# Five numbers and one condition in the virtual clock of a fused S4D and MLP-mixer kernel

## The chip, the cores and the metric

The kernel runs on one core of a Trainium2 chip. That core has a matrix engine (TensorE, called PE in the profile), a vector engine (VectorE, DVE), a scalar engine (ScalarE, ACT), GpSimd (POOL) and a queue engine (SyncE, SP), each with its own instruction stream; they meet at semaphores only. DMAs are issued from SP, ACT and POOL. The metric is the device time of one execution in microseconds, as the median of several runs.

## The reference

```python
xn = _layernorm(x)                              # x: 2048 tokens x 576 channels
s  = irfft(rfft(xn^T) * rfft(K))^T + xn * D_skip   # K: S4D kernel, 576 channels, 128 states, 2048 long
h  = gelu_tanh(_layernorm(xn) @ w1 + b1)        # 576 -> 4608
g  = silu(h @ w2 + b2)                          # 4608 -> 576
return x + s * g
```

Everything is fp32, and the channel convolution is as long as the sequence.

## The kernel before, in words

There are two bodies of work. The MLP ("mlp") is cut into 48 slots. The 4608 hidden features form 12 groups of 384, the 2048 tokens form four blocks of 512; the first half of the kernel takes the token blocks 0 and 1 through all 12 groups, the second half the blocks 2 and 3. A slot is one group for one block of 512 tokens. It has 11 positions on PE: three tiles of layer 1 (L619, 14 matmuls of 512 columns each, since every fp32 product is made of three fp32r products of high and low parts), and eight positions of layer 2 (L682; 12, 6, 6, 12, 18 and 18 matmuls of 288 columns in the order of the trace, 72 in all). Behind each layer 1 tile ACT makes Gelu (L655), ACT rounds it to the high part `hh` (L658) and DVE subtracts to get the low part `hl` (L661); layer 2 reads both. Layer 2's sums are added into `acc` by DVE (L692).

The second body is the S4D convolution ("s4d"). 36 steps make the convolution's kernel: tables of sines and magnitudes on ACT and DVE (L917 to L957; the two sines of a step are L934 and L936), then 64 small matmuls on PE ("KG", L996). Six chunks of 96 channels are then convolved by transforms: "X1" (L1108, twice a chunk), "K1" (L1139, twice), "S2" (the second stage, L1167, four times), "INV" (the inverse step, L1210, twice) and "I1" (L1236, once), with ACT and DVE work between them. I1's result goes to DRAM (`s_s`, L1245).

At the end the output x + s*g is made in two ways. For tokens of blocks 0 and 1, `combine_load` (L721 to L723) brings u, s and g back in `row` tiles by three POOL DMAs, `combine` multiplies and adds on DVE (L729, L730), and POOL issues the stores (L733). This is done in two rounds: one for the first 384 channels when four of the six chunks are done, and one for the last 192 channels in three sets (three, three and two blocks of tokens) when the last chunk is done; the sets follow one another in one line of steps. For blocks 2 and 3, `finish` works straight from `acc` in the last two slots: ACT (L765), then DVE (L770 or L772 and L776, then L780), then the store (L782). `row` tiles have four buffers.

The order of all instructions on all engines is made while the program is traced, by the class `Order`, a list scheduler with a virtual clock. Its clock has one time per engine (`t`). Work on PE of the MLP is placed by `unit`; all other work stands in "lines", each a queue of `step`s with an engine, a duration, marks that it needs and perhaps a latest start (`by`). `advance` runs, up to the PE clock, whatever can start earliest. A step of a line may run only if it ends before the next urgent step of its engine has to start (`soon`, from the `by` times of Gelu, `hh`, `hl` and `acc`, which `hidden_by`, `add_by` and `look_ahead` work out from the list `LEN` of the durations of a slot's positions). An urgent step itself (Gelu and what follows it, and the evacuation of a KG that rode with another unit) isn't tested. ACT's functions need tables: Gelu and tanh one, the sines another, exp and sqrt others. `take` adds 1.28 to a step that has to change the table; the test in `advance` adds 1.28 or 2.56 for a step that itself needs a table. A load of a table is an instruction on ACT (ACT_TABLE_LOAD) in the trace. A step with no engine stands for a DMA; its duration is the time after which the next step of its line may start.

The S4D units are put between MLP positions by `pe_turns`, at set places of a slot, when the virtual clock has their inputs ready. Units of X1, K1, S2 and I1 are spread out: `END = 1000.0` is the virtual time at which the last is to be placed, and the number of units left sets the gap between them. A KG whose inputs are ready rides with such a unit (`ride`). Between slots, a "pair" of two half-height matmuls (L602) may take the place of one matmul in each of the first and third tile.

The durations of the planner are constants: X1 (used for X1 and K1), S2, INV, I1 and KG at L1026, L1 (one layer 1 tile, three for each slot) at L1354, and the waits of DMA steps, among them the one of `combine_load` at L1519.

Of the kernel before, what the change touches and what calls it, by code (L numbers as in the profile page):

```python
# [19 lines left out]
NT = 16  # L20
# [19 lines left out]
def dve(n):  # L40
    return 0.075 + 0.00104 * n
# [10 lines left out]
class Order:  # L52
# [85 lines left out]
    def advance(self, horizon):  # L138
        while True:
            best = None  # L140
            soon = dict(self.next)
            for u in self.urgent:
                st = u[1][0]
                k = (max(u[0], self.t[st["eng"]]), 0)
                if u[0] <= horizon and (best is None or k < best[0]):
                    best = (k, u, None)
                for st in u[1]:
                    soon[st["eng"]] = min(soon.get(st["eng"], 1e9), st["by"])
            for x in self.lines:
                if x["steps"] and x["steps"][0]["by"] < 1e9:  # L150
                    st = x["steps"][0]
                    soon[st["eng"]] = min(soon.get(st["eng"], 1e9), max(st["by"], self.t[st["eng"]] + st["dur"]))
            for n, x in enumerate(self.lines):
                h = self.head(x)
                if h is None or h[0]["eng"] == "PE":
                    continue
                st, r = h
                if st["eng"] is None:
                    k = (max(r, 0), 1 + n)
                    if r > horizon:  # L160
                        continue
                else:
                    e = st["eng"]
                    b = max(self.t[e], r)
                    d = st["dur"]
                    if st["tbl"]:
                        d += 1.28 * (1 + (st["tbl"] != self.tbl))
                    if b > horizon or b + d > soon.get(e, 1e9) + st["late"]:
                        continue
                    k = (b, 1 + n)  # L170
                if best is None or k < best[0]:
                    best = (k, None, x)
            if best is None:
                break
            if best[1] is not None:
                self.go(best[1])
            else:
                self.run(best[2])
            self.pin()
# [26 lines left out]
def step(eng, dur, fn, need=(), mark=None, cv=0, at=0.0, late=0.0, tbl=None, by=1e9):  # L206
    return dict(eng=eng, dur=dur, fn=fn, need=tuple(need), mark=mark, cv=cv, at=at, late=late, tbl=tbl, by=by)
# [3 lines left out]
def mixer_kernel(ctx, tc, u, log_a_real, a_imag, c_real, c_imag, log_dt, d_skip, w1, b1, w2, b2,  # L211
# [394 lines left out]
    def layer1(g, tb, i):  # L606
        h, lo, r1, r2 = W[1]
        c = slice(i * P, (i + 1) * P)
        if i < 2 and i not in BEGUN:
            Q1[i] = bank2(mx(i))  # L610
        q = Q1[i % 2][:, i // 2]
        ops = []
        for a, b in ((h, XH), (h, XL), (lo, XH)):
            ops += [(a[:, kb, c], b[:, kb, tb]) for kb in range(KB)]
        ops.append((r1[:, c], XR[:, tb]))
        if i not in BEGUN:
            ops.append((r2[:, c], XR[:, tb]))
        for j, (a, b) in enumerate(ops):
            nc.tensor.matmul(q, a, b, start=j == 0 and i not in BEGUN, stop=j == len(ops) - 1, skip_group_check=True)  # L619
        return hidden(g, tb, i, q)  # L620

    def first_layer1(i):


        h, lo, r1, r2 = W[1]
        if i != 1:
            Q1[i] = bank2("mxb" if i else "mxa")
        q = Q1[2][:, 0] if i == 2 else Q1[0][:, i]
        pairs = [(h, XH, 0), (h, XH, 1), (h, XL, 0), (h, XH, 2), (h, XL, 1), (h, XH, 3), (h, XL, 2), (h, XL, 3)]

        if i != 1:
            for j, (a, b, kb) in enumerate(pairs):
                for k in ((0, 1), (2,))[i // 2]:
                    nc.tensor.matmul(Q1[k // 2 * 2][:, k % 2], a[:, kb, k * P:(k + 1) * P], b[:, kb, 0],
                                     start=j == 0, stop=False)
        c = slice(i * P, (i + 1) * P)
        for kb in range(KB):
            nc.tensor.matmul(q, lo[:, kb, c], XH[:, kb, 0], start=False, stop=False)
        for r in (r1, r2):
            nc.tensor.matmul(q, r[:, c], XR[:, 0], start=False, stop=r is r2)  # L640

        return [hidden(0, 0, k, Q1[k // 2 * 2][:, k % 2]) for k in ((), (0, 1), (2,))[i]]
# [75 lines left out]
    def combine_load(b, n, c0, c1):  # L718
        m = c1 - c0
        r = [sb.tile([P, D], F32, name="row", bufs=NROW)[:, :n * m].rearrange("p (i d) -> p i d", i=n) for _ in range(3)]  # L720
        nc.gpsimd.dma_start(r[0], u_s[:, b:b + n, c0:c1])  # L721
        nc.gpsimd.dma_start(r[1], s_s[:, b:b + n, c0:c1])
        nc.gpsimd.dma_start(r[2], g_s[b:b + n, :, c0:c1].rearrange("i p d -> p i d"))  # L723
        XS[b] = r

    def combine(b, n, c0, c1):

        x, s, g = XS[b]
        nc.vector.tensor_mul(s, s, g)  # L729
        nc.vector.tensor_add(x, x, s)  # L730
        for i in range(n):
            for y, o in enumerate(rows_at(out, b + i, c0, c1)):
                nc.gpsimd.dma_start(o, x[64 * y:64 * y + 64, i])  # L733
# [289 lines left out]
        return behind  # L1023


    X1, S2, INV, I1, KG = 1.5, 1.75, 2.15, 3.05, 1.03  # L1026

    def chunk(c):

# [242 lines left out]
    el, wl2, wl, nl2, pl, pl2, nl, ml, ml2, xl, wx, c3, c2, c1, c4, kl, tl, sl, vl, gl, odl, fl = [od.line() for _ in range(22)]  # L1272
# [78 lines left out]
    od.pin()  # L1351


    L1 = 14 * 0.2315  # L1354
    LEN = [L1] * G + [3 * n * 0.132 + 0.02 for n in (4, 2, 2, 4, 3, 3, 3, 3)]

    T0 = 12.5
# [96 lines left out]
    def wmark(n, which):  # L1454

        per = KB + 1 + G
        a = n * per + (0 if which == 1 else KB + 1)
        return [("w", k) for k in range(a, a + (KB + 1 if which == 1 else G))]
# [23 lines left out]
    for k in range(8):  # L1482
        gl["steps"].append(step("POOL", 0.7, lambda k=k: part.update({k: load_f2(k)}), mark=("f2", k),
                                need=[("f2c", k - 2)] if k > 1 else ["turns"]))
        fl["steps"].append(step(None, 4.5, lambda: None, need=[("f2", k)]))
        for f in range(2):
            fl["steps"].append(step("ACT", act(256), lambda k=k, f=f: part[k](f), mark=("f2c", k) if f else None,
                                    need=[("f2s", k - 1)] if k and k % 2 == 0 else []))
# [26 lines left out]
    def end_line():  # L1515
        for c, c0, c1, sets in ((NCH - 3, 0, CE, [(b, 1) for b in range(8)]), (NCH - 1, CE, D, [(0, 3), (3, 3), (6, 2)])):
            for b, n in sets:
                a = (b, n, c0, c1)
                ml["steps"].append(step(None, 10.0, lambda a=a: combine_load(*a), need=[("st", c), ("u", NT - 1)]))  # L1519
                ml["steps"].append(step("DVE", 2 * dve(n * (c1 - c0)), lambda a=a: combine(*a)))  # L1520
                ml["steps"].append(step(None, 4.0, lambda: None))

# [46 lines left out]
    later(mid - 2, G, lambda: (parts_in(0), turn_in(1)))  # L1569
    later(mid - 1, G, lambda: parts_in(1))  # L1570
    later(NSLOT - 10, 4, end_line)
    later(NSLOT - 2, 0, lambda: wx["steps"].append(step(None, 0.0, load_identity)))
    for k in range(8):
# [40 lines left out]
    for slot in range(NSLOT):  # L1614
# [5 lines left out]
        for pos in range(NPOS):  # L1620
            if pos < G:
                need = wmark(n, 1) + [("x", tb)]
                if pos == 0:
                    od.force(lambda: all(m in od.marks for m in need))

                    if slot in (1, 2 * NG + 1):
                        od.marks["x", tb] -= 2.3
                cell = []
                od.unit(lambda: cell.extend([layer1(g, tb, pos)] if slot else first_layer1(pos)),
                        L1 * (14 - (pos in BEGUN)) / 14 if slot else L1 * (22, 6, 14)[pos] / 14, need)  # L1630
                if pos == 2:
# [16 lines left out]
            else:  # L1648
                j, terms, last, hid = l2_terms(pos - G)
                need = [wmark(n, 2)[i] for i in hid] + [("h", slot, i) for i in hid]  # L1650
# [17 lines left out]
                elif last:  # L1668
                    add = cell[0]
                    chain = [step("DVE", dve(D), lambda: add(0, 2), mark=("acc", slot, j), by=add_by(pos, j))]  # L1670
                    if final:
                        x = el if slot < NSLOT - 1 else od.line()
                        st = finish(b, 0, D, slot == NSLOT - 1, nc.gpsimd if slot == NSLOT - 1 and j > 1 else nc.sync)
# [69 lines left out]
```

## Time and profile before

| what | value |
|---|---|
| median of 3 runs | 1102.57 us (1101.76 to 1102.64) |
| the profiled execution's own time | 1102.84 us |
| its span, first to last instruction | 1101.0 us |
| granted TensorE clock, mean | 0.999 |
| PE busy | 1090.1 us |
| DVE busy | 892.8 us |
| ACT busy | 725.7 us |
| Gelu's table loads (at L655) | 39 |
| table loads at L934 and L936 | 27 and 7 |

A row of the timeline has the start in us, the busy time, engine, line and operation, output and input, the count, and in brackets the idle time before it with what ended it. A row of the waits has the engine and line that waited, what it waited for, the total in us, the number of times and the longest. Matmuls are pipelined: consecutive matmuls of 288 columns start 0.13 us apart, though each is listed with 0.29 us, so a late start is read from the distance of two starts.

### The profile page before, as it was taken

The numbers are of one execution on the slowest core, as the hardware profiler recorded it, in microseconds if no ns is written. First come the engines' busy times: TensorE is split into PE (matmuls) and PEld (weight loads), VectorE is DVE, ScalarE is ACT, GpSimd is POOL, SyncE is SP. The second block draws the span as 40 slices with busy tenths as digits, with TensorE's granted clock in tenths as the row PEclk, the third lists the DMA queues.
The fourth block names the chain that finished last, engine by engine and source line by source line (L and its number), as shares of the span: only waits on it lengthen the run. The fifth ranks groups of instructions, "written<-read, shape, count | busy, mean of one in ns | idle before, by whom it ended". The sixth has DMA issues, their size and how long they took to land.

```text
span 1101.0 us, 27023 instructions
## 1 busy us (share of the span) xinstructions
PE 1090.1 (99%) x11445; PEld 954.5 (87%) x11445; DVE 892.8 (81%) x1298; ACT 725.7 (66%) x1109; POOL 184.1 (17%) x255
## 2 busy tenths in 40 slices
PE   9999999999999999999999999999999999999997
PEld 7989899898888898888888888888888888888897
DVE  7798677979888889889997988988798986666356
ACT  6585699876848685586947669577666766335233
POOL 4566201071110100001100010000100012110320
PEclk9999999999999999999999999999999999999999
DMA  8846755745542333344723334242333425563543
GB/s 227 236 147 152 236 160 193 214 87 150 160 147 75 67 97 95 99 103 128 169 58 90 85 89 100 53 119 64 92 76 91 146 64 163 131 179 100 161 129 87
DMA packets 139649, 138.22 MB, mean 126 GB/s; under 512 B 88952, under 2 KB 105016, under 8 KB 138952
## 3 DMA queue, kind: packets, MB, share of 16 engines
q1 hardware_dynamic: 124664, 85.49, 29.7%
q0 software_dynamic: 14384, 50.27, 14.7%
q8 instruction: 89, 1.46, 0.6%
q10 hardware_dynamic: 480, 0.74, 0.3%
q14 instruction: 32, 0.26, 0.1%
HBM read 102.17 MB, written 36.63 MB: 126 GB/s over the span
## 4 chain that ended last, share of the span: by engine, by line
PE 87%; DVE 4%; ACT 3%; DMA 2%; SPq 2%; issue 1%; POOL 0%; ACTq 0%; DVEq 0%; POOLq 0%
PE mxb L682 19%; PE mxa L682 19%; PE mxb L619 18%; PE mxa L619 18%; PE cv L1167 3%; PE cv L996 3%; PE cv L1210 2%; PE cv L1139 1%; PE cv L1108 1%; PE cv L1236 1%; SPq L810 1%; DMA row<-g_s 1%; DMA w<-in_A_u_dram 1%; SPq L385 1%; ACT h L655 0%
## 5 line engine op out<-in xcount | busy, mean ns | idle before, releaser
L661 DVE TENSOR_TENSOR hl<-h,hh 128x512 fp32r<-128x512 f32 x144 | 98.7, 688 | 104.1 <-ACT hh L658 103.8
L682 PE MATMUL mxa<-w2h,hh 128*128 128x288 f32 x573 | 171.2, 299 | 2.0 <-DVE acc L692 1.0
L682 PE MATMUL mxb<-w2h,hh 128*128 128x288 f32 x576 | 171.3, 297 | 0.0
L682 PE MATMUL mxb<-w2h,hl 128*128 128x288 f32 x576 | 170.6, 296 | 0.6 <-DVE hl L661 0.5
L682 PE MATMUL mxa<-w2h,hl 128*128 128x288 f32 x573 | 169.2, 295 | 0.4 <-DVE hl L661 0.4
L682 PE MATMUL mxb<-w2l,hh 128*128 128x288 f32 x576 | 169.5, 294 | 0.0
L682 PE MATMUL mxa<-w2l,hh 128*128 128x288 f32 x573 | 168.6, 294 | 0.0
L682 PEld LDWEIGHTS mxa<-w2h,hh 128*128 128x128 f32 x573 | 107.6, 188 | 9.8 <-issue 4.2
L655 ACT ACTIVATE h<-mxa,b1t 128x512 f32<-128x512 f32 x73 | 50.1, 687 | 94.8 <-PE mxa L619 93.6
L682 PEld LDWEIGHTS mxb<-w2h,hh 128*128 128x128 f32 x576 | 108.1, 188 | 4.9 <-issue 1.8
L682 PEld LDWEIGHTS mxb<-w2h,hl 128*128 128x128 f32 x576 | 108.1, 188 | 1.6 <-DVE hl L661 1.5
L682 PEld LDWEIGHTS mxb<-w2l,hh 128*128 128x128 f32 x576 | 108.2, 188 | 0.7
L682 PEld LDWEIGHTS mxa<-w2l,hh 128*128 128x128 f32 x573 | 107.6, 188 | 0.6
L682 PEld LDWEIGHTS mxa<-w2h,hl 128*128 128x128 f32 x573 | 107.5, 188 | 0.6 <-DVE hl L661 0.6
L692 DVE TENSOR_TENSOR acc<-mxa,acc 128x576 f32<-128x576 f32 x87 | 65.3, 751 | 36.4 <-PE mxa L682 36.2
L898 POOL DMA_DIRECT2D par<-par_s x36 | 27.5, 765 | 394.6 <-DVE mg L942 317.9
L658 ACT ACTIVATE hh<-h 128x512 fp32r<-128x512 f32 x144 | 90.8, 631 | 3.7
L655 ACT ACTIVATE h<-mxb,b1t 128x512 f32<-128x512 f32 x71 | 48.8, 687 | 65.3 <-PE mxb L619 62.7
L692 DVE TENSOR_TENSOR acc<-mxb,acc 128x576 f32<-128x576 f32 x88 | 66.1, 751 | 19.5 <-PE mxb L682 19.3
L619 PE MATMUL mxa<-XH,w1h 128*128 128x512 f32 x284 | 78.3, 398 | 0.0
L619 PE MATMUL mxb<-XH,w1h 128*128 128x512 f32 x280 | 77.9, 400 | 0.0
L619 PE MATMUL mxa<-XL,w1h 128*128 128x512 f32 x284 | 76.1, 390 | 0.0
(266 smaller groups left out, 2481.5 us busy)
## 6 DMA issues: line engine op xcount, KB each, us to landing
raw<-in_B_w_dram SPq DMA_DIRECT2D x72, 288.0 KB, 3.5
raw<-in_B_w_dram SPq DMA_DIRECT2D x96, 192.0 KB, 3.5
par_s<-A POOLq DMA_DIRECT2D x4, 2160.0 KB, 9.0
par<-par_s POOLq DMA_DIRECT2D x36, 240.0 KB, 3.7
f2t<-f2q SPq DMA_DIRECT2D x24, 256.0 KB, 3.3
g2t<-g2p SPq DMA_DIRECT2D x24, 256.0 KB, 3.8
bias<-XR SPq DMA_DIRECT2D x42, 128.0 KB, 3.5
raw<-in_B_w_dram SPq DMA_DIRECT2D x48, 96.0 KB, 3.6
```

What stands on the lines that cost most here:

```text
L385: queue.dma_start(XT[b], tok(u, b))
L619: nc.tensor.matmul(q, a, b, start=j == 0 and i not in BEGUN, stop=j == len(ops) - 1, skip_group_check=True)
L655: nc.scalar.activation(t, q, AF.Gelu_apprx_tanh, bias=b1t[:, k:k + 1], scale=1.0)
L658: LAST[0] = nc.scalar.activation(hh[:, i], t, AF.Copy)
L661: nc.vector.tensor_sub(hl[:, i], t, hh[:, i].bitcast(F32))
L682: nc.tensor.matmul(q[:, dh, :288], a[:, i, c], b[:, i, d], start=i == 0 and k == 0 and not alone, stop=i == G - 1 and k == 2)
L692: nc.vector.tensor_add(o, q[:, dh:dh + n, :288], b)
L810: nc.sync.dma_start(r[32 * g:32 * g + 32].rearrange("c (b n) -> c b n", n=32), dram(src[k], 32 * g, [[N, 32], [32 * N, D // 32], [1, 32]]))
L898: nc.gpsimd.dma_start(PAR[b].rearrange("p (g i) k -> p g (i k)", g=4), dram(par_s, (b // 3 * 48 + b % 3 * 4) * NPAR, [[D * NPAR, P], [12 * ...
L996: nc.tensor.matmul(q[32 * g:32 * g + 32, i // 2, i % 2 * 64:i % 2 * 64 + 64], U[:, ri, 4 * g + i, :], v[:, ri, 4 * g + i, :], start=ri == ...
L1167: nc.tensor.matmul(Q[i][32 * q:32 * q + 32, f, ri::2], m[r, 4 * i + q, 32 * ri:32 * ri + 32], A2[r, 4 * p + 2 * i + q // 2, :, :, q % 2], ...
L1210: nc.tensor.matmul(QI[q // 2][64 * f:64 * f + 64, q % 2, i], MAT["g2t", p + i // 2][r, i % 2, f, ri], YS[p + i // 2][0][r, i % 2, ri, f], ...
```

## The change

The condition: the test of a step of a line on ACT that itself needs no table counts 1.28 more while the table in the virtual clock isn't Gelu's. The numbers: X1 1.50 to 1.48, S2 1.75 to 1.73, INV 2.15 to 1.98, KG 1.03 to 1.04; a matmul of layer 1 from 0.2315 to 0.2275, thus a tile from 3.241 to 3.185; and the wait behind `combine_load` from 10 to 13.

```diff
@@ -165,6 +165,8 @@
                     d = st["dur"]
                     if st["tbl"]:
                         d += 1.28 * (1 + (st["tbl"] != self.tbl))
+                    elif e == "ACT" and self.tbl != "gelu":
+                        d += 1.28
                     if b > horizon or b + d > soon.get(e, 1e9) + st["late"]:
                         continue
@@ -1023,7 +1025,7 @@
-    X1, S2, INV, I1, KG = 1.5, 1.75, 2.15, 3.05, 1.03
+    X1, S2, INV, I1, KG = 1.48, 1.73, 1.98, 3.05, 1.04
@@ -1351,7 +1353,7 @@
-    L1 = 14 * 0.2315
+    L1 = 14 * 0.2275
     LEN = [L1] * G + [3 * n * 0.132 + 0.02 for n in (4, 2, 2, 4, 3, 3, 3, 3)]
@@ -1516,7 +1518,7 @@
-                ml["steps"].append(step(None, 10.0, lambda a=a: combine_load(*a), need=[("st", c), ("u", NT - 1)]))
+                ml["steps"].append(step(None, 13.0, lambda a=a: combine_load(*a), need=[("st", c), ("u", NT - 1)]))
```

No instruction's shape or operands change; what changes is the order in which the instructions stand on the engines, and what follows from it. The two added lines move the line numbers behind L167 by two; this text keeps the numbers from before.

## The prediction

> **What bounds the kernel now.** First the page: the span and the engines' busy time.
>
> ```profile
> span 1101.0 us, 27023 instructions
> PE 1090.1 (99%) x11445; PEld 954.5 (87%) x11445; DVE 892.8 (81%) x1298; ACT 725.7 (66%) x1109; POOL 184.1 (17%) x255
> ```
>
> PE is busy all but 10.9 us. So the time is PE's own stream of matmuls, plus its late starts, plus a tail after the last matmul. Then the waits of PE:
>
> ```profile
> PE mxa L1298 <- POOL XL L1291: 1.3, 1, 1.3
> PE mxa L682 <- DVE acc L692: 1.0, 1, 1.0
> PE mxb L682 <- DVE hl L661: 0.5, 2, 0.3
> PE mxa L682 <- ACT h L655: 0.5, 2, 0.2
> ```
>
> The first is the start of the kernel and doesn't change. The others, in the middle, are small. By distances of starts (0.13 us where nothing waits) I find late starts in layer 2 at 47, 338, 458, 480, 552, 670, 742 and 933 us, 4.6 us in all. That, with about 0.1 us for each restart, is all that a better order can win in the middle. Third, the timeline at three of these places:
>
> ```profile
> 334.51 0.37 ACT L1001 ACTIVATE kt<-cv 128x256 f32<-128x256 f32 x1
> 335.36 1.10 ACT L923 ACTIVATE w<-w 128x1040 int32<-128x1040 f32 x1
> 336.47 1.28 ACT L655 ACT_TABLE_LOAD   x1
> 337.77 0.69 ACT L655 ACTIVATE h<-mxa,b1t 128x512 f32<-128x512 f32 x1
> 337.99 0.29 PE L682 MATMUL mxb<-w2h,hl 128*128 128x288 f32 x1
> 338.51 0.41 PE L682 MATMUL mxa<-w2h,hh 128*128 128x288 f32 x1 [0.23 <-ACT h L655]
> 339.56 0.29 PE L682 MATMUL mxb<-w2l,hh 128*128 128x288 f32 x1
> 339.90 0.40 PE L682 MATMUL mxb<-w2h,hl 128*128 128x288 f32 x1
> 480.80 0.40 PE L682 MATMUL mxa<-w2h,hh 128*128 128x288 f32 x1 [0.24 <-ACT h L655]
> 482.35 0.40 PE L682 MATMUL mxb<-w2h,hl 128*128 128x288 f32 x1 [0.22 <-DVE hl L661]
> 667.85 0.38 ACT L1001 ACTIVATE kt<-cv 128x256 f32<-128x256 f32 x1
> 668.25 1.28 ACT L655 ACT_TABLE_LOAD   x1
> ```
>
> At 336.47 Gelu's table is loaded in the middle of a slot, because a sine stood before; the load and the step ahead of it make the third Gelu late, and PE starts 0.52 - 0.13 = 0.39 us late at 338.51 (the bank is still being read) and 0.34 - 0.13 = 0.21 late at 339.90 (`hl`). At 480 it is the same with 0.40 and 0.38, at 670 with 0.25 and 0.23: 1.86 us in three places. In the order of before, exactly three of Gelu's 39 loads stand after the second hidden tile of a slot; these are the three.
>
> Three more late starts are of other kinds:
>
> ```profile
> 741.87 0.40 PE L682 MATMUL mxa<-w2h,hh 128*128 128x288 f32 x1 [0.42 <-issue]
> 552.91 0.40 PE L682 MATMUL mxa<-w2h,hh 128*128 128x288 f32 x1 [1.00 <-DVE acc L692]
> 931.51 0.56 DVE L729 TENSOR_TENSOR row<-row 128x384 f32<-128x384 f32 x1 [2.02 <-DMA row<-g_s]
> 933.32 0.40 PE L682 MATMUL mxa<-w2h,hl 128*128 128x288 f32 x1 [0.36 <-DVE hl L661]
> ```
>
> At 552 `acc` came late on DVE (1.15 us by starts); at 742 it was 0.49, with no engine named. At 931 DVE stood 2.02 us in front of a `combine` whose loads hadn't landed, with an `hl` queued behind it: 0.52 us on PE.
>
> **The change, part by part.** From 1102.84 us, the profiled execution's own time (span 1101.0 and 1.8 around it); the median of the runs is 0.27 lower.
>
> *PE's own work.* The two programs have the same matmuls on PE, 15 pairs each. In the changed order 28 instead of 29 KGs ride, and one more run of foreign matmuls cuts the MLP. A cut costs the first matmul behind it some 0.1 us (0.38 against 0.29 in the row of 31.57 below). A ride saves one cut. I take +0.2, between 0 and 0.4.
>
> *The condition.* With it, L923 (1.10) couldn't have stood at 335.36 ahead of a load. But L1001 is urgent and isn't tested; at 667.85 it alone made Gelu late, with the load, by 0.25. The changed order has four of Gelu's loads after the second tile (slots 25, 32, 33, 39), and three have an L1001 between sine and load. The three old places cost 1.86, with six restarts some 2.4; the new four at best nothing, at worst what 670 cost (0.48 and two restarts, 0.7) times three, 2.1. I take 1.3, so the condition wins 1.1, between 0.3 and 2.4. Three more loads of each table (39 to 42 at L655, 7 to 10 at L936) are 6 x 1.28 = 7.7 us of ACT, hidden in its 375 idle us as long as none stands ahead of a late Gelu.
>
> A rule speaks against the size of the reserve. The Trainium skill, "ScalarE: Activation LUTs", section "What ACT_TABLE_LOAD costs", adds a drain of about 1.38 us to the load's 1.28. By that rule 1.28 is half of what is needed, and four loads could come late by 1.38 each, an estimated 5.5 us more from that page. The trace disagrees: load at 336.47, Gelu at 337.77.
>
> *The wait of 13.* DVE isn't put in front of a `combine` so early: the 0.52 at 933 and a restart go, -0.6 (between -0.6 and 0).
>
> *PE's durations.* A tile is now 3.185 in the clock and 144 of them make 8.1 us less, INV 12 x 0.17 = 2.0 less, X1 and S2 together 48 x 0.02 = 1.0 less. The trace has 1.85 to 3.2 us for these pieces; the clock is now nearer to it. But `END` stays at 1000, so S4D's units stand later relative to the MLP by up to 11 us: the last I1 moves from slot 44, before layer 2, to the same place of slot 45, one slot (19 us) later. This moves the last round of `combine`, and its three waits now are 39 instead of 30. In the changed order of DVE its first two sets stand in the hidden tiles of slots 46 and 47, and the third, L729 and L730, is the last thing on DVE, behind the last L780. On POOL its four stores are the last DMAs.
>
> **The tail** is therefore what I work out most closely:
>
> ```profile
> 1069.26 0.55 DVE L729 TENSOR_TENSOR row<-row 128x384 f32<-128x384 f32 x1
> 1069.84 0.56 DVE L730 TENSOR_TENSOR row<-row 128x384 f32<-128x384 f32 x1
> 1070.70 2.12 POOL L733 DMA_DIRECT2D out_dram<-row  x4 [9.36 <-DVE row L730]
> 1096.08 0.45 DVE L770 SCALAR_TENSOR_TENSOR A<-A,h 128x288 f32<-128x288 f32 x1
> 1096.57 0.46 DVE L780 TENSOR_TENSOR w<-w,A 128x288 f32<-128x288 f32 x1
> 1096.19 1.38 ACTq L782 DMA_DIRECT2D out_dram<-w  x2
> out_dram<-row POOLq DMA_DIRECT2D x16, 48.0 KB, 2.2
> out_dram<-w ACTq DMA_DIRECT2D x2, 72.0 KB, 2.5
> ```
>
> Before, this set was stored at 1070.70, hidden by slot 46. The last L780 ends at 1097.03, the last store is issued by ACT at about 1097.06 and lands 2.5 later, 1099.5. After: L729 starts at 1097.0, L730 0.58 later, ending at 1098.15; POOL begins 0.30 behind it (1070.40 to 1070.70), 1098.45; the fourth of its DMAs begins three quarters of 2.12 later, 1100.05, and lands after 2.2, 1102.25. That is +2.7, and what follows the landing follows it as before. POOL is the slower issuer here and each queue end adds something, so I take +3.0. The low bound is 2.2, if the four stores land as fast as the fastest of that line (1.8), the high one 5.4 if as slow as the slowest:
>
> ```profile
> DMA to landing us min/median/max: 1.8/2.3/5.0
> ```
>
> The third set holds three of four `row` buffers while L765 of slot 47 needs them in turn: the third L765 must wait for L770 of the second tile, and moves from 1092.41 to about 1093.1, ending 1093.8, when its L770 started anyway. Nothing is queued behind it that is due earlier, so I cost it at 0.1 within the 3.0.
>
> **New late starts.** One is certain enough to compute. In slot 0 the 16 transposes move nine matmuls later, and an L692 moves between the XL subtractions:
>
> ```profile
> 29.91 1.91 PE L502 MATMUL cv<-f2t,row 128*128 128x128 f32 x16
> 31.57 0.38 PE L682 MATMUL mxb<-w2h,hh 128*128 128x288 f32 x1
> 34.04 0.60 PE L502 MATMUL cv<-f2t,row 128*64 128x128 f32 x4
> 30.98 2.07 ACT L506 ACTIVATE XH<-cv 128x512 fp32r<-128x512 f32 x4 [4.86 <-PE cv L502]
> 32.10 2.48 DVE L512 TENSOR_TENSOR XL<-cv,XH 128x512 fp32r<-128x512 f32 x4 [1.24 <-ACT XH L506]
> ```
>
> Nine times 0.133 is 1.2: XH from 32.2, the first two L512 from 33.3 to 34.5. The last four transposes reuse their bank and wait until then: 34.04 becomes 34.5 to 34.6. +0.5; DVE's waits at 47 us may shrink by as much, so +0.3 (0 to 0.9). Another is slot 32, where DVE now has six table products between the second and third `hl`:
>
> ```profile
> L942 DVE TENSOR_TENSOR mg<-par 128x1024 f32<-128x1024 f32 x72 | 66.9, 952 | 0.7
> L951 DVE TENSOR_TENSOR w<-w,mg 128x1024 f32<-128x1024 f32 x36 | 43.8, 1216 | 1.6 <-ACT w L936 1.6
> L953 DVE TENSOR_TENSOR w<-w,mg 128x1024 f32<-128x1024 f32 x36 | 43.7, 1213 | 0.0
> L955 DVE TENSOR_TENSOR w<-w,mg 128x512 f32<-128x512 f32 x36 | 24.5, 681 | 0.0
> ```
>
> Here L951, L953, L955, L957 and both forms of L942 (mean of 0.95, so 1.90 for the two) make about 1.22 + 1.21 + 0.68 + 0.68 + 1.90 = 5.7, and less where starts overlap; PE gives this `hl` an S2, a tile and 18 matmuls, about 1.8 + 3.2 + 2.4. With what stands before, it is late by 0 to 0.8. The kind seen at 552, 742 and 458 (1.15, 0.49, 0.16) isn't treated by the change; some 40 slots are mixed anew, so I expect its 1.8 again, and 0.8 for slot 32 and its like; between -1.8 and +4.
>
> Sum of the middle: -1.1 - 0.6 + 0.3 + 0.8 = -0.6. All: 1102.84 + 0.2 + 3.0 - 0.6 = 1105.4, and 1105.2 for the median.
>
> **Rivals.**
> - *The middle wins what the tail loses.* All three old load places clean (-2.4), 933 gone (-0.6), 552 not repeated (-1.2), nothing new but slot 0 (+0.3): -3.9 with +3.2 gives 1101.9. For it: the clock is nearer to the trace and the causes are the ones named. Against: three untested L1001 still stand ahead of mid-slot loads.
> - *Faster.* The tail is cheap (2.2), and the middle wins all of its 4.6 with a dozen restarts, 5.7: 1102.57 + 2.2 + 0.2 - 5.7 = 1099.3. Against: it needs every late start gone.
> - *A new place in the middle dominates.* A DVE-bound stretch like slot 32 or 552 loses 1 to 4 us again, as 552 did with 1.15 at once: 1105.2 + 3 = 1108. For it: DVE is busy 81% and S4D is packed more tightly into the slots 36 to 45.
> - *The order changes but nothing moves in time*: 1102.6. Against: the last L730 and its stores stand behind the last L780, whatever the clock says.
>
> **How the numbers follow.** Forecast (tail, even middle; 1103 to 1107): 0.5. Middle wins back (1101 to 1103): 0.2. Dominating new place (1107 to 1110): 0.2. Faster: 0.06. Nothing moves: 0.04. 0.2% is 2.2 us, so faster ends at 1100.4 and slower begins at 1104.8, which cuts the forecast: 0.34 of its 0.5 above, with the new place 0.54; same 0.37; faster 0.09, with 0.03 from the second case. The range is 1101.2 to 1109.0.
>
> **What would show it.** In the changed profile: L729 and L730 last on DVE, four POOL stores after them, the span ending about 7 us after the last L780 and not 4.0 (1101.0 less 1097.03); no L923 ahead of a mid-slot load; PE's waits for L655 and L661 at four mid-slot loads of 0.3 us or less; a late L502 at 34 us; no DVE wait of 2 us at an L729. Wrong, if the third set's loads land early and its DVE work is hidden, or if one PE wait above 2 us shows in the middle.

## The result, and the profile after

The changed kernel takes 1107.12 us (median of six runs, 1106.19 to 1110.02), the kernel before 1102.43 beside it (six runs, 1101.57 to 1102.85): a ratio of 1.0048, with a 95% interval of 1.0035 to 1.0061. It is slower by 4.7 us by the two medians, and by 5.3 by the ratio, which is taken over all runs; 2.6 were forecast. The profiled execution took 1108.48 us, of which the span is 1106.7.

The lines of the changed kernel have numbers higher by two behind L167; from here on they are given as the profile of each kernel has them. The page of the changed kernel, its head and engines:

```profile
span 1106.7 us, 27025 instructions
...
PE 1090.7 (99%) x11445; PEld 953.8 (86%) x11445; DVE 892.8 (81%) x1298; ACT 735.3 (66%) x1115; POOL 184.4 (17%) x255
```

PE's own work is nearly what it was (1090.7 against 1090.1 us busy), so the 5.7 us of the span are waits and tail. Three marks split them: the first start of L619 (slot 1), the end of the last matmul, and the end of the span. Start: 34.39 before, 34.78 after, +0.4. Middle, from there to the last matmul: 1060.55 and 1062.95, +2.4. Tail: 6.10 and 8.99, +2.9. Half of the loss is where the prediction put all of it, and the other half is in the start and the middle, which together were to win 0.6, less 0.2 for PE's work. PE's waits in the changed kernel:

```profile
PE mxa L684 <- DVE hl L663: 1.9, 2, 1.7
...
PE mxa L684 <- DVE acc L694: 1.2, 2, 0.7
PE cv L1110 <- ACT pr L1087: 0.7, 1, 0.7
PE cv L504 <- DVE XL L514: 0.5, 1, 0.5
```

By distances of starts the late starts are 7.5 us now, 4.6 before. The last row is the one computed for slot 0. The first is slot 32, and the third is a place that no rival had. The tail first, in the timeline of DVE and POOL:

```profile
1099.39 0.46 DVE L782 TENSOR_TENSOR w<-w,A 128x288 f32<-128x288 f32 x1
1099.77 0.55 DVE L731 TENSOR_TENSOR row<-row 128x384 f32<-128x384 f32 x1
1100.35 0.56 DVE L732 TENSOR_TENSOR row<-row 128x384 f32<-128x384 f32 x1
...
1101.20 2.10 POOL L735 DMA_DIRECT2D out_dram<-row  x4 [2.22 <-DVE row L732]
```

This is the tail as it was worked out, row for row: the last set's two steps behind the last L782, POOL 0.29 us behind them, four stores, and the span's end 6.85 us after the end of that L782 (4.0 before).

Slot 32 is the place that was to cost 0 to 0.8 and cost 1.86. The timeline there, first ACT, then DVE, then PE:

```profile
730.79 1.28 ACT L938 ACT_TABLE_LOAD   x1
732.09 1.09 ACT L938 ACTIVATE w<-w 128x1040 f32<-128x1040 f32 x1
733.20 1.28 ACT L657 ACT_TABLE_LOAD   x1
734.49 0.69 ACT L657 ACTIVATE h<-mxb,b1t 128x512 f32<-128x512 f32 x1
735.21 0.63 ACT L660 ACTIVATE hh<-h 128x512 fp32r<-128x512 f32 x1
...
731.62 0.68 DVE L944 TENSOR_TENSOR mg<-par 128x512 f32<-128x512 f32 x1
733.21 1.23 DVE L953 TENSOR_TENSOR w<-w,mg 128x1024 f32<-128x1024 f32 x1 [0.90 <-ACT w L938]
...
736.81 1.23 DVE L944 TENSOR_TENSOR mg<-par 128x1024 f32<-128x1024 f32 x1
737.95 0.68 DVE L663 TENSOR_TENSOR hl<-h,hh 128x512 fp32r<-128x512 f32 x1
...
740.01 0.75 DVE L694 TENSOR_TENSOR acc<-mxa,acc 128x576 f32<-128x576 f32 x1
...
738.69 0.40 PE L684 MATMUL mxa<-w2h,hl 128*128 128x288 f32 x1 [1.71 <-DVE hl L663]
```

One sine (L938) stands alone between two Gelus and costs two table loads. DVE waits 0.90 for it; then four products of the table (L953 to L959, 733.21 to 736.78) and one L944 run in front of `hl`, whose input was ready at 735.84. The 0.90 come from the sine's own load. By an estimate from these rows, without its 1.28 us the sine would have ended at about 731.9, before DVE was done with L944 at 732.3. The second load is followed by Gelu 0.01 us later, and the sine ends 0.02 us ahead of it. The drain that was weighed in the prediction (the Trainium skill, "ScalarE: Activation LUTs", section "What ACT_TABLE_LOAD costs") doesn't show here either.

The new place is X1, at 829.7 us. ACT's and SP's waits, and the timeline of ACT, SP and PE:

```profile
ACT xt L1078 <- DMA xc<-xn_s: 8.8, 3, 3.5
...
SPq L541 <- DVE w2l L571: 111.0, 40, 8.5
```

```profile
814.54 2.10 ACT L1078 ACTIVATE xt<-xc 128x768 f32<-128x768 f32 x1
...
826.67 2.12 ACT L1078 ACTIVATE xt<-xc 128x768 f32<-128x768 f32 x1 [3.50 <-DMA xc<-xn_s]
...
819.27 0.33 SPq L541 DMA_DIRECT2D raw<-in_B_w_dram  x1
819.65 3.84 SPq L1043 DMA_DIRECT2D xc<-xn_s  x4
...
829.71 0.61 PE L1110 MATMUL cv<-pr,f2t 64*128 64x384 f32 x4 [0.75 <-ACT pr L1087]
```

The second `xc` of a chunk goes into the buffer that the first `xt` frees, at 816.64. Its load is issued at 819.65 only, behind a raw weight load, one of the 40 that wait in SP's queue until DVE has split an earlier one. ACT goes in order, stands 3.50 us before L1078, and passes that on. There are three such waits (1.76, 3.52 and 3.50 us). The profiled execution of before has none, though two of its pairs of `xt` start closer than these would without the wait (8.5 us apart from 372.67 on and 7.9 from 795.94 on, against 12.13 - 3.50 = 8.6).

### The profile page after: what moved, and what is told of

Read it like the earlier page. It is cut to its first block, busy times and chain, and to the rows that moved or that the text cites. A ratio compares the mean times of both kernels' runs of the same rounds, so it can differ in the third digit from the quotient of the medians.

```text
span 1106.7 us, 27025 instructions
## 1 busy us (share of the span) xinstructions
PE 1090.7 (99%) x11445; PEld 953.8 (86%) x11445; DVE 892.8 (81%) x1298; ACT 735.3 (66%) x1115; POOL 184.4 (17%) x255
## 4 chain that ended last, share of the span: by engine, by line
PE 90%; DVE 4%; ACT 1%; SPq 1%; DMA 1%; issue 1%; POOL 0%; POOLq 0%; DVEq 0%; ACTq 0%
PE mxb L684 20%; PE mxa L621 19%; PE mxa L684 19%; PE mxb L621 18%; PE cv L1169 3%; PE cv L998 3%; PE cv L1212 2%; PE cv L1238 2%; PE cv L1141 1%; PE cv L1110 1%; PE mxa L1300 1%; DMA row<-y_s 1%; DMA xc<-xn_s 1%; DVE acc L694 1%; SPq L474 1%
```

## The experiments

Each run was compared with the kernel before on the same chip. Middle and tail are those of its one profiled execution, as defined above; before has 1060.55 and 6.10. One execution is a small sample. Where the order is the same, a late start can come and go. At 47 us before has a late `hl` of 0.42, and e7 and e8, with before's order there, have none; e9 has 0.43 there, and the changed kernel, e5 and e10, with the same order there, have none.

| run | median, us | before beside it | ratio, 95% interval | middle | tail |
|---|---|---|---|---|---|
| changed kernel | 1107.12 | 1102.43 | 1.0048 (1.0035 to 1.0061) | 1062.95 | 8.99 |
| e1 last set early | 1106.45 | 1101.34 | 1.0039 (1.0027 to 1.0052) | 1062.85 | 7.03 |
| e2 xc on ACT's queue | 1125.83 | 1101.34 | 1.0222 (1.0203 to 1.0241) | 1078.17 | 9.11 |
| e3 hl first in slot 32 | 1109.82 | 1101.34 | 1.0071 (1.0058 to 1.0083) | 1061.68 | 8.99 |
| e4 the three together | 1124.78 | 1101.34 | 1.0211 (1.0197 to 1.0225) | 1077.85 | 6.79 |
| e5 xc behind xt on SP | 1105.52 | 1101.27 | 1.0037 (1.0024 to 1.0049) | 1059.25 | 8.99 |
| e6 condition alone | 1106.30 | 1101.27 | 1.0040 (1.0026 to 1.0054) | 1064.17 | 6.00 |
| e7 L923 held (on before) | 1103.11 | 1101.27 | 1.0016 (1.0007 to 1.0025) | 1061.81 | 6.09 |
| e8 wait of 13 alone | 1101.62 | 1101.27 | 1.0001 (0.9993 to 1.0010) | 1059.75 | 6.09 |
| e9 e5 and the sets early | 1103.90 | 1102.88 | 1.0008 (1.0000 to 1.0017) | 1061.29 | 6.10 |
| e10 e5, sets at 10, sine held | 1100.62 | 1102.88 | 0.9974 (0.9965 to 0.9984) | 1057.27 | 5.81 |
| e11 durations alone | 1133.54 | 1102.88 | 1.0275 (1.0260 to 1.0290) | 1073.90 | 23.26 |
| e12 e11 with END 970 | 1110.64 | 1101.38 | 1.0084 (1.0071 to 1.0098) | 1066.63 | 7.14 |

The expectations of e1, e2 and e5 write L1080 for the `xt` step that the profiles list as L1078.

### The tail: e1 and e9

e1 alters one wait of the planner:

```diff
-step(None, 13.0, lambda a=a: combine_load(*a), ...)
+step(None, 13.0 if n != 2 else 3.0, lambda a=a: combine_load(*a), ...)
```

> The changed kernel with one step of the planner altered: the load wait of the last combine set is 3.0 instead of 13.0. Every matmul, ACT and SP instruction keeps its place; on DVE the pair L731/L732 of the last set moves from behind the last L782 to twelve instructions before it, on POOL one output store of slot 47 moves behind the set's four. Theory (the tail is this set's two DVE steps and four POOL stores behind the last L782): in the changed kernel the span ends 6.85 us after the end of the last L782, in the kernel before 4.0; with the set early the 2.8 go, so 2.6 to 3.0 us less than the changed kernel, about 1104.3, and the last matmul stays where it was, near 1097.7. Rival (the end of the span is set by the landing of whatever is stored last, or the set's loads come as late as its DVE steps stood): under 1.0 us less, and DVE or POOL waits for the loads at L731. A smaller loss of its own is possible: the 1.1 us of DVE now stand ahead of hidden tiles of slot 47, at most 0.5 on PE.

The span is 2.0 us shorter, not 2.8: tail 7.03. By the ratios it is 1.0 us (1.0048 to 1.0039) with overlapping intervals, so the times alone don't show it. The timeline of e1 shows the rest:

```profile
1087.27 0.73 POOL L723 DMA_DIRECT2D row<-u_s  x1
...
1092.15 0.56 DVE L731 TENSOR_TENSOR row<-row 128x384 f32<-128x384 f32 x1 [1.63 <-DMA row<-g_s]
...
1100.28 0.46 DVE L782 TENSOR_TENSOR w<-w,A 128x288 f32<-128x288 f32 x1
```

The end of the span is again 3.9 us after the last L782, as before, but that L782 ends 0.89 later than in the changed kernel. The loads stood on POOL behind the second set's stores, landed too late, and DVE, on which the whole end hangs, stood 1.63 us in front of L731. So the theory holds for the order, and the rival's part (late loads) took a third back. e9 makes all three sets earlier (8.0 for 13.0), upon e5:

> The kernel of e5 (xc issued right behind xt) with the load wait of the three last combine sets at 8.0 instead of 13.0, so that the loads of all three are traced earlier: on DVE the last set now stands 17 instructions ahead of the last L782, one L767 moves by three places on ACT, PE's order is the same. Theory (the tail of the changed kernel is the set behind the last L782, and in e1 0.9 us of it came back only because the set's loads were issued at 1087 us behind the stores of the second set): the span ends 4.0 us after the end of the last L782 and about 6.1 us after the last matmul, against 8.99 in e5; 2.5 to 3.0 us less than e5, a ratio of 1.0005 to 1.0015 to the kernel before. Rival (loads so early are not landed, DVE stands 1 to 2 us at an L731 with an hl queued behind it, as at 931 us in the kernel before): 1.5 us less than e5, with a PE wait of 0.5 us or more for hl behind 1020 us.

The tail is 6.10, and the ratio falls from 1.0037 to 1.0008. Both agree with the theory (2.5 to 3.0 us less, a ratio of 1.0005 to 1.0015). A part of the rival came too, not at `hl` but at `acc`: 0.99 us by starts at 1073 us. It is half of the 2.0 us by which this middle is longer than e5's; 0.46 at 549 us and 0.43 at 47 us come from places where the order is e5's.

### The late xc: e2, e4 and e5

e2 moves the issue of `xc` from SP to ACT, every instruction otherwise in its place:

```diff
-                    nc.sync.dma_start(XC[i][...], dram(xn_s, ...))
+                    nc.scalar.dma_start(XC[i][...], dram(xn_s, ...))
```

> The changed kernel with its xc loads issued by ACT instead of SP (48 issues), every other instruction of every engine in its place. Theory (in the changed order the xc loads stand in SP's queue behind raw weight loads that wait for DVE's splits, land late, and ACT, which goes in order, stands 8.8 us before L1080 in three places and passes that on to PE): ACT's three waits at L1080 for the xc DMA (1.76, 3.52 and 3.50 us) fall below 0.5 each, PE's late starts at 548, 551, 685 to 687, 830 and 837 us (0.66, 0.24, 0.82, 1.47, 0.81) shrink to 0.5 in all; 3 to 4 us less than the changed kernel, 1103.1 to 1104.1. Rival 1 (the transfer itself is slow: it is a gather of short rows, or it is held up by other transfers): the loads are issued earlier but ACT still waits over 1 us at each place, gain under 1.0. Rival 2 (the 48 issues cost ACT as much as they win, ahead of Gelus): new waits of PE for ACT h, gain under 1.0 or a loss.

A plain miss: some 19 us slower than the changed kernel (0.0174 between the ratios) where 3 to 4 were to be won. ACT's row, and PE behind it:

```profile
195.89 7.04 ACTq L1043 DMA_DIRECT2D xc<-xn_s  x4
202.97 0.38 ACT L1003 ACTIVATE kt<-cv 128x256 f32<-128x256 f32 x1 [6.46 <-DMA xc<-xn_s]
...
203.99 0.40 PE L684 MATMUL mxa<-w2h,hh 128*128 128x288 f32 x1 [2.97 <-ACT h L657]
```

Issuing these four DMAs held ACT for 7.04 us, with Gelu behind them. Of 48 such issues the median is 0.58 us and the longest 3.32. That is rival 2, at places where the changed kernel had no stall at all. e4, which contains this edit, is drowned by it:

> The edits of the three other runs of this call together: last combine set early, xc loads on ACT's queue, third hl of slot 32 first. Theory (three separate causes that add): 2.8 + 3.5 + 1.8 = 8.1 us less than the changed kernel, about 1099.0, so faster than the kernel before by 2.5 to 4. Rival (the causes overlap, or what is won in the middle is eaten by other late starts that were hidden behind them): 4 to 6 us less, 1101 to 1103, no faster than the kernel before.

Its tail (6.79) agrees with e1's, and its sum says nothing on whether the three add. e5 leaves the issue on SP and changes the order of SP's queue only:

```diff
-                nc.scalar.activation(T["x"], get(), AF.Copy)
+                nc.scalar.activation(T["x"], get(), AF.Copy); i + 1 < CH // 48 and load(i + 1)
-                four.append(step(None, 5.0, lambda: load(i + 1), mark=("xl", c, i + 1)))
+                four.append(step(None, 5.0, lambda: None, mark=("xl", c, i + 1)))
```

> The changed kernel with SP's queue alone reordered: the load of a chunk's second xc is issued directly behind the xt (L1080) that frees the buffer, in five places ahead of a raw weight load or a par load that stood ahead of it; every other engine's order is the changed kernel's. The issue of its four DMAs is not made cheaper (about 3.8 us on SP at L1043, and 7.0 us on ACT where ACT issued them). Theory (the queue's order, a blocked head, is what makes xc late): at 527, 671 and 815 us xc is issued 3 to 11 us earlier, ACT's waits at L1080 for xc fall from 7.5 to 8.8 us to under 2.5 in all, and PE's late starts at 548, 685 to 687 and 830 us go or shrink to 0.3 each; 1.5 to 2.5 us less than the changed kernel, a ratio of 1.0025 to 1.0035 to the kernel before. Rival (what is won on xc is lost on the raw loads, which now wait behind 3.8 us of issuing): DVE or ACT waits for raw at L574 or L571 of 1 us or more appear, and PE waits for w1h, w1l, w2h or w2l; no gain or a loss.

The place at 816 us in e5, where `xt` now follows `kt` with no wait and X1's wait at 829.7 is gone:

```profile
815.88 2.27 SPq L1043 DMA_DIRECT2D xc<-xn_s  x4
818.48 3.21 SPq L541 DMA_DIRECT2D raw<-in_B_w_dram  x4
...
822.26 2.10 ACT L1078 ACTIVATE xt<-xc 128x768 f32<-128x768 f32 x1
```

No wait of ACT for `xc` is left. Matmul by matmul against the profiled changed kernel, the late starts at 685 to 687 (0.82), 829.7 and 830.7 (1.36) and 837 us (0.81) are gone; at 548 an `acc` is now late by 0.62 more. The middle is 3.7 us shorter, 1.3 below that of before. By the runs the gain is smaller: 1.2 us by the ratios (1.0048 to 1.0037, just above the theory's 1.0025 to 1.0035), 0.4 us by the medians, and the two intervals overlap. The rival came in part. ACT and DVE in e5:

```profile
534.71 0.68 ACT L574 ACTIVATE w2h<-raw 128x576 fp32r<-128x576 f32 x1 [1.49 <-DMA raw<-in_B_w_dram]
...
545.39 0.70 DVE L479 STREAM_TRANSPOSE row<-row 64x512 f32<-64x512 f32 x1 [2.26 <-DMA row<-y_s]
```

With `xc` ahead of them on SP, ACT waits up to 1.49 us for a raw load (0.6 in the changed kernel), and the last `y_s` loads are issued at 540.56 and not at 538.35; the `acc` at 549 us stands on DVE behind the transpose that waits for them. It is late by 1.28, 1.74 and 1.43 us in e5, e9 and e10, which share this queue, and by 0.66, 0 and 0 in the changed kernel, e1 and e3, which have the old one.

The three waits for `xc` are there again in e1 and e3 (7.5 and 7.2 us in all), but they aren't the changed order's alone. In the profiled executions of e7 and e8, which have the order of before there, ACT waited once for `xc`, for 6.9 and 4.1 us.

### Slot 32: e3 and e10

e3 keeps all as it is, but puts `hl` ahead of four steps on DVE:

```diff
+        f = lambda g, *a: (lambda: HELD.append(lambda: g(*a))) if (b, g, *a) in ((26, weigh, 1),
+            (26, weigh, 2), (26, weigh, 3), (27, mags, 0)) else (lambda: g(*a))
...
+            nc.vector.tensor_sub(hl[:, i], t, hh[:, i].bitcast(F32)); [HELD.pop(0)() for _ in list(HELD)]
```

> The changed kernel with one instruction of one engine moved: in slot 32 the third hl (L663) stands ahead of L955, L957, L959 and L944 on DVE instead of behind them; all other engines are as they were. Theory (PE's 1.86 us at 738.69 are this stack of DVE work): hl can begin when hh ends, at about 735.85, and PE needs it at 736.8; the 1.86 go, 1.7 to 1.9 us less, about 1105.3, and nothing comes late behind it, since the work behind hl ends when it did. Rival (the Gelu with its table load at 733.20 is what makes hl late): hh ends too late for PE and a stall of 0.5 or more stays at this place. Second rival: the four steps now come late for the KG or the kk chain behind them, and PE loses the 1.86 again within two slots; the time is the changed kernel's within 0.5.

```profile
734.46 0.69 DVE L663 TENSOR_TENSOR hl<-h,hh 128x512 fp32r<-128x512 f32 x1 [1.44 <-ACT hh L660]
...
740.13 0.75 DVE L694 TENSOR_TENSOR acc<-mxa,acc 128x576 f32<-128x576 f32 x1
...
740.94 0.40 PE L684 MATMUL mxa<-w2h,hh 128*128 128x288 f32 x1 [3.25 <-DVE acc L694]
```

In these rows of e3 `hl` is in time, and PE's 1.86 us at 738.69 go; 16 matmuls later PE waits 3.25 for `acc`, which stands behind the same stack. Against the changed kernel PE is 1.9 ahead and then 1.4 behind where it was. The second rival is shown in kind and not in size: it had the changed kernel's time within 0.5 us, and e3 is some 2.5 us slower by the ratios, with intervals that just overlap. Some 1.4 of the 3.25 are e3's own, since `hl`, put so early, makes DVE stand 1.44 for `hh`. A milder order would have won little: in the changed kernel this `acc` ends at 740.76, 0.16 ahead of the matmul that uses it at 740.92. So an `hl` in time wins some 0.2 us as long as `acc` stays behind the stack; this is an estimate from the rows, and an order with `acc` further ahead wasn't run. So e10 takes the sine out, upon e5, with the last sets' wait at 10:

```diff
-                 step("ACT", act(SB * NV), f(sin, 1), mark=("sin", b, 1), tbl="sin")],
+                 step("ACT", act(SB * NV), f(sin, 1), mark=("sin", b, 1), tbl="sin", at=738 if b == 26 else 0.0)],
```

> The kernel of e5 with the wait of the three last sets at 10.0 and with the second sine of table 26 held back (planned not ahead of 738) until it no longer stands alone between two Gelus in slot 32. The order of everything behind slot 31 is mixed anew: Gelu's table is loaded 39 times and the second sine's 7 times, as in the kernel before, one Gelu load stands behind the second tile of a slot (slot 25), the last set stands 14 instructions ahead of the last L782. Theory (the lone sine with its two loads, and the table products that it releases at once, made DVE the bound of slot 32; the stall can't be moved within the slot, as e3 showed, but goes with the sine): no PE wait above 1.0 us behind 560 us, 1.9 us less in the middle and 2.9 less in the tail than e5; about 1099.5 where the kernel before has 1101.3, a ratio of 0.9975 to 0.9995. Rival (the same DVE work comes out somewhere else in slots 33 to 45, since S4D's table work is as much as before): a stall of 1 to 2 us at another place, ratio 1.000 to 1.002.

Its ratio is 0.9974 (0.9965 to 0.9984): faster than the kernel before by 0.26%, and than the changed one, which had 1.0048; it is just below the theory's 0.9975 to 0.9995. Against e5, as the theory has it, the middle is 2.0 us shorter (1.9 were expected) and the tail 3.2 (2.9). In the waits of e10's PE nothing over 1.0 is left behind 560 us; the `acc` is the one at 549 us:

```profile
PE mxa L684 <- DVE acc L694: 1.3, 1, 1.3
```

Against e9 the middle is 4.0 us shorter; slot 32 is 1.9 of it, 1073 us 1.0. What the new order behind slot 31 does beyond that wasn't taken apart.

### The parts alone: e6, e8, e11 and e12

> The kernel before with the new condition alone (durations and the wait of 10 as they were). In its order Gelu's table is loaded 42 times and the sine's at L936 to L938 11 times (before 39 and 7), five Gelu loads stand after the second tile of a slot (slots 15, 32, 33, 39, 41), the last I1 stands in slot 45, and the last combine set stands twelve instructions ahead of the last L780, so not in the tail. Theory of the prediction (the condition wins at the three old places and loses little at the new ones): 0.3 to 2.4 us less than before, about 1101. Rival (the condition makes single sines stand between Gelus and packs DVE's table steps behind them, as in slot 32 of the changed kernel, and this costs more than the three old places): 1 to 4 us more than before, with a PE wait above 1.5 us in slot 32.

The rival, and a little more than its 1 to 4 us: 5.0 by the two medians, 4.4 by the ratio, and without any tail (6.00). In the waits of e6's PE, and on DVE in slot 23:

```profile
PE mxa L684 <- DVE hl L663: 1.9, 2, 1.7
```

```profile
526.31 0.69 DVE L957 TENSOR_TENSOR w<-w,mg 128x512 f32<-128x512 f32 x1
526.91 0.69 DVE L663 TENSOR_TENSOR hl<-h,hh 128x512 fp32r<-128x512 f32 x1
```

The sine of slot 32 stands alone in this order too (1.87 us late at 740.9), and slot 23 is of the same kind: table products ahead of `hl`, PE late by 1.20 us at 527.65. None of the three old table-load stalls is left. So the condition does what it says, and the order that follows from it loses more.

> The kernel before with the load wait of the combine sets at 13.0 instead of 10.0 and nothing else; its order differs from that of before only behind 917 us. Theory of the prediction: DVE's 2.02 us in front of a combine at 931 go and with them PE's 0.52 at 933; 0.5 to 0.6 us less than before, the tail unchanged (4.0 us from the end of the last L780 to the end of the span), since the last set stands 19 instructions ahead of the last L780. Rival: the DVE wait only moves to another combine or to the tail, and the time is that of before within 0.2 or more.

```diff
-                ml["steps"].append(step(None, 10.0, lambda a=a: combine_load(*a), ...))
+                ml["steps"].append(step(None, 13.0, lambda a=a: combine_load(*a), ...))
```

The late start at 933 is gone from e8's trace, but the ratio is 1.0001 (0.9993 to 1.0010): an effect of 0.5 us is within this interval, so neither theory is excluded. The profiled execution is 1.2 us shorter in its span than the profiled one before, and has a late start of 0.85 at 870 behind the wait for `xc` named above; 0.4 of the 1.2 is the late start at 47 us, ahead of all that e8 changes.

> The kernel before with the new durations alone (X1, S2, INV, KG and L1), without the condition and with the wait of 10. In its order Gelu's table is loaded 43 times, the second sine's 11 times; three Gelu loads stand behind the second tile of a slot, two of them (slots 16 and 22) behind an L923 as in the kernel before; the last I1 stands in slot 46 and the last L730 two instructions ahead of the last L780. Theory of the prediction (the durations do nothing to the middle and cost a tail through the later last I1): the middle as before within 1 us, the tail 1 to 2.2 us longer; 1.0 to 3.0 us more than before. Rival 1 (the durations help the middle by 1 us or more, and it was the condition that lost it): within 1 us of before. Rival 2 (any later or denser packing of S4D costs, with lone sines in new slots, as with the condition alone): 4 us or more above before with a PE wait above 1.5 us.

It costs 31 us by the medians, far beyond the theory and the first rival. The second rival's bounds are met, but its lone sine isn't what PE waits for longest: the longest wait of PE, 3.9 us at 485, is for an `acc` that stands behind a transpose for whose DMA DVE waited 6.58 us. PE's last matmul comes 14 us later, and 23.26 us follow it. On POOL, I1's result:

```profile
1082.14 0.94 POOL L1245 DMA_DIRECT2D s_s<-pr  x1 [85.73 <-ACT pr L1244]
1083.50 0.90 POOL L1245 DMA_DIRECT2D s_s<-ys  x1 [0.41 <-ACT ys L1244]
```

S4D ends here 25 us before PE does, and everything that reads `s_s` is crowded behind it. e12 has the same durations and END at 970, so that the last I1 comes in slot 45:

> The kernel of e11 (the new durations alone) with END at 970 instead of 1000; the order written is another one: the last I1 in slot 45 instead of 46, the last KG in slot 42 instead of 43, the last L730 eight instructions ahead of the last L780 instead of two, one Gelu load behind an L923 in a slot's middle (slot 16) instead of two. Theory (of the 30 us of e11 the tail's 17 come from S4D's end alone: s_s was stored at 1083 us, some 25 us ahead of the last matmul, and everything that reads it, 16 output tiles, came behind): the tail is 6 to 8 us again instead of 23.3, so at least 15 us less than e11; what is left against the kernel before is the middle's, 2 to 13 us. Rival 1 (one slot earlier is not enough, the last stage stays late): the tail stays above 12 us. Rival 2 (the middle's 13 us were this order's accident, two long stalls and the slower clock behind them, and not the durations): the whole is within 4 us of the kernel before.

The tail is 7.14, the whole 1.0084: 21 us less than e11 by ratios. The theory holds for the tail. The middle keeps 6.1 us, and one stall in slot 21 alone is longer. The waits of e12's PE and its timeline there:

```profile
PE mxb L682 <- DVE acc L692: 7.1, 1, 7.1
```

```profile
476.70 8.65 SPq L472 DMA_DIRECT2D row<-y_s  x12
...
482.60 0.71 DVE L477 STREAM_TRANSPOSE row<-row 128x512 f32<-128x512 f32 x1 [6.35 <-DMA row<-y_s]
...
487.04 0.75 DVE L692 TENSOR_TENSOR acc<-mxb,acc 128x576 f32<-128x576 f32 x1
```

DVE stood 6.35 us in front of a transpose whose DMA hadn't landed, with `acc` behind it. e11 has 3.9 us at the same place. Whether the durations as such cost anything stays open: each order they gave has an accident of its own.

### The reserve itself: e7

e7 is the kernel before, with L923 of two tables moved behind the third Gelu of slots 15 and 21, and its L926 behind `hl`:

```diff
+            go = lambda: nc.scalar.activation(T["w"][:, 0].bitcast(I32), T["w"][:, 1], AF.Copy); HELD.append(go) if b in (10, 17) else go()
...
+            nc.vector.tensor_sub(hl[:, i], t, hh[:, i].bitcast(F32)); [HELD.pop(0)() for _ in list(HELD)]
```

> The kernel before with the step L923 of tables 10 and 17 held back behind the third Gelu and hh of slots 15 and 21 (and its L926 on DVE behind that slot's hl); nothing else moves. Theory (the 1.10 us of L923 ahead of the table load make the Gelu at 337.77 and the one at 480 late): the Gelus come 1.1 us earlier, PE's late starts 0.39 and 0.21 at 338 to 340 and 0.40 and 0.38 at 480 to 482 go, 1.4 us less than before, up to 1.8 with the restarts. Rival (the load itself, or what stands ahead of it, is what counts; or DVE's chain behind the held L926 comes late for a KG): 0.5 or less is won, with stalls at the same places or one slot later.

```profile
338.85 1.24 DVE L926 TENSOR_TENSOR w<-w 128x1040 f32<-128x1040 f32 x1 [0.70 <-ACT w L923]
...
341.42 0.75 DVE L692 TENSOR_TENSOR acc<-mxb,acc 128x576 f32<-128x576 f32 x1
...
342.22 0.40 PE L682 MATMUL mxb<-w2h,hh 128*128 128x288 f32 x1 [1.47 <-DVE acc L692]
```

Against before, the four late starts go with just the sizes they had: 0.39, 0.21, 0.40 and 0.38. Then 1.63 and 1.64 come back some 4 us later in each slot: L926 waits for the later L923, and `acc` stands behind it. It is slower by 1.8 us. So L923 did cause the old stalls, and its place was still the cheaper one.

## Why the prediction was right, and where it was wrong

The sign held, the time lies in the range, and the tail is as forecast; the middle had the wrong sign. The tail's 3 us alone give the sign. That the time lies in the range is in part luck: start and middle were some 3 us off, and the range, 7.8 us wide, isn't added up from the bounds of its terms.

- *The tail* (+3.0; +2.9 by the profiled executions). The rows came nearly as worked out: the last store landed 2.5 us later behind the last L782 than before (4.75 against 2.27), where 2.7 were expected, and the span ended 2.11 us behind the landing and not 1.75, which is the 0.3 laid on POOL and the queue ends. (By the prediction's own rows the bounds are 2.3 and 5.5 rather than 2.2 and 5.4.) e9 shows that the tail goes when the sets are earlier. The third L767 that waits for the single `row` left was harmless.
- *Slots 0 and 1* (+0.5 at 34 us against 0.42 at 47). The first came, 0.52 of idle time at 34.42 (0.68 by starts), and is there in each run with this order. That nothing is late at 47 can't be laid on the change: this late start comes and goes in either order, as said above.
- *PE's own work* (+0.2). Its busy time rose by 0.6, but a granted clock of 0.998 for 0.999 is part of this figure, so the term can't be told apart.
- *"The condition wins 1.1".* This step failed: with e6, the condition alone costs some 4 us. The loads that the working priced cost less than the 1.3 set for them: slot 25 lost 0.19 with the load and an untested L1001 ahead, slots 33 and 39 nothing. But a load ahead of a late Gelu is not the price of a lone sine. In slot 32 Gelu's load is hidden, and what costs is on DVE: the table products that the sine releases, and DVE's wait for the sine, which its own load makes late.
- *"Slot 32 itself 0 to 0.8"* was mis-sized: 1.86. The working set the sum of the products, 5.7, against the 7.4 us that PE gives, with no waiting among them; DVE stood 0.90 us for the sine and started the rest at 733.21. The other 1.0 is a little above the 0.8.
- *`xc` was not in the sum at all.* In the trace of before ACT never waited for it, and nothing in the orders of PE, ACT and DVE tells of it; it comes from SP's queue. In the profiled execution it carried about 3 us. Taking it away gave 1.2 us by the ratios, with overlapping intervals, and made an `acc` later at 549.
- *The wait of 13* (-0.6): the late start went, a gain can't be told from none.
- *The durations.* The prediction laid the late I1 on them and on END at 1000. With END at 990 the order of the changed kernel is the same instruction for instruction, and the condition alone also has the last I1 in slot 45. So END was not what held it, and the durations needn't have been. What the planner's choice hung on instead is not shown.
- *The rivals.* "A new place dominates" (1108, from 1107 to 1110) came nearest to what the middle did, and 1107.12 lies just inside it and just outside the forecast's 1103 to 1107; slot 32 was named in it, `xc` was not.

The parts do not add: condition, durations and wait alone have ratios of 1.0040, 1.0275 and 1.0001, together 1.0048.

## What to carry to other kernels

A planner's constant is judged by the order it writes, not by its nearness to the trace: the condition alone cost 0.4% and the durations alone 2.8%, though both bring the clock nearer to the trace. Another order within a full slot only moved the wait (e3, e7); taking work out of the slot removed it (e10). And when an order changes, read each DMA queue for what its head waits on, since a load behind a blocked one is late without any engine's order showing it.

## What the runs showed of the hardware

A long stall of PE can cost more than its length. After a stall the granted clock may fall for some four microseconds. The windows of e2 behind the stall of 2.97 at 203.99, of e1 around that of slot 32, and of e3 in its 3.25:

```profile
204.00:208.00 4.00, 4.00 (x19) 0.58 0.29 50
```

```profile
736.00:740.00 4.00, 2.68 (x15) 0.82 0.00 0
740.00:744.00 4.00, 4.00 (x51) 0.76 0.00 0
```

```profile
738.00:740.00 2.00, 0.00 (x0) 1.00 0.00 0
740.00:742.00 2.00, 1.06 (x8) 1.00 0.00 0
```

The columns are the window, its length, PE's busy time and matmuls, the granted clock, DMA share and GB/s. In e1 the loss of clock is 4 x 0.18 and 4 x 0.24, 1.7 us; by starts PE falls 1.4 us behind the changed kernel there, three quarters of the stall itself; in the changed kernel's profiled execution the same stall cost no clock, nor did the longer one of e3's. It differs from execution to execution: e3's five runs go from 1107.69 at a mean clock of 0.998 to 1111.48 at 0.994. The Trainium skill, "TensorE: Matmul & The Clock Gate", section "What's actually happening", has the clock halve after an idle window of about 3.4 us that runs free of the kernel. The part of chance and the half clock agree (0.50 in the lowest windows of 2 us); that 1.7 us of idleness can be enough is what e1's trace shows.

The issue of a DMA can hold its engine: `xc`'s 96 KB took 0.31 to 3.32 us each on ACT and, in the changed kernel, up to 6.07 on SP.
